# Output matmuls in one run per tile shape, and PSUM banks of their own for the first three chunks, in a linear-attention and two-layer MLP kernel

## The chip, the cores and the metric

The kernel runs on one core of a Trainium2 chip. The metric is the device time of one execution in microseconds (us); a lower time is better. Each figure for a whole kernel is the median of several executions. The profiles come from one execution each.

## The reference

Four batches of eight heads with 768 steps of 48 channels go through a gated linear recurrence. Its output, as 3072 tokens of 384 channels, goes through two gated MLPs with a width of 1536; the second normalizes its input first. Everything is float32.

```python
for t in range(S):
    state = alpha[:, :, t, :, None] * state + np.einsum('bhd,bhe->bhde', k[:, :, t], v[:, :, t])
    y[:, :, t] = np.einsum('bhd,bhde->bhe', q[:, :, t], state)
x = y.transpose(0, 2, 1, 3).reshape(B * S, H * D)
# first MLP
g = x @ w_gate;  x = (g * sigmoid(g) * (x @ w_val)) @ w_out
# second MLP: the same with its own weights, on x / rms(x) * rms_g
```

## The kernel before

**The recurrence in chunks.** The 768 steps of each of four batches are cut into six chunks of 128 steps: 24 chunks `n` in all, batch after batch within a step range, so that chunk `n` continues the state of chunk `n - 4`. A chunk works on all eight heads at once, as four pairs `p` with a half `h` each on partitions 0 to 63 and 64 to 127. Inside a chunk, the work goes by levels `LEVELS = (1, 2, 4, 8, 16, 32, 64)`, called l0 to l6 below. `merge` multiplies the decays into q and k in place on VectorE (DVE), level by level. `copy_qk` (ScalarE, ACT) copies what a level needs. `scores` (TensorE, PE) forms q k^T of a level as 16 matmuls with a tile of 64 rows and 32 columns. `masks` (DVE) and `copies_p` (ACT) bring the scores to SBUF. `outputs` adds, for each level, four matmuls with a tile of 128 rows and 32 columns and eight matmuls with a tile of 64 rows and 32 columns into the chunk's output in PSUM; chunks from n = 4 on also take in the old state that way (`Sd`, 128 rows; `Sc`, 64 rows). `own_terms` starts this output with three transposes of `yn`. For chunks up to n = 19, four transposes of k (into `kp`, copied to `kt` by ACT) and 16 matmuls in `kv` form the k^T v that `state` adds to the state. A matmul of float32 small tiles shows as two records in the trace. Chunks 0 to 5 use all levels, chunks from 6 on start at l2 and compute the first steps directly on DVE (`direct_ops`), which ends in `yn` after two DMAs through DRAM.

**Steps and slots.** A chunk has steps T = 0 to 19. A new chunk starts every 12 slots, so that step T of chunk n runs in the same slot as step T - 12 of chunk n + 1, and the older chunk comes first in the slot. In `chunk`, scores of l0 to l3 are at T = 6, masks of l0 to l2 at T = 7 and of l3 at T = 8, scores of l4 to l6 at T = 9, their masks and copies at T = 10, transposes of k at T = 12, their copy at T = 13, `own_terms` and the outputs of l0 to l3 at T = 14, `kv` and the outputs of l4 to l6 at T = 16, and `split_x` and `state` at T = 17 and 18. `split_x` writes the chunk's output from PSUM into the MLP's input (L375, L379 on ACT, L381 on DVE). Every engine runs its instructions in the order of this program.

**PSUM.** There are eight banks. Three are the tile `Y`, the others are `g`, `v`, `o0`, `o1` and `o2` of the MLP, one buffer each. The first 128 columns of the three banks of `Y` hold the chunk's output. The other columns hold the scores, the transposed k and k^T v of every chunk.

**The MLPs.** Tokens are in blocks of 3, 3, 3, 3, 4, 4 and 4 chunks in the first MLP and six blocks of 4 in the second. `mlp_points` walks over the blocks and over 12 slices f of the width; each (block, f) has three pieces: `g` (L612), `v` (L612) and `o` (L653), where `o` belongs to the slice before. Chunks 0 to 2 run before the first block, with T = 6 of chunk 3 ahead of the first `g`. After that, the slots of the chunks of the next block are spread over the pieces: one slot after each piece in blocks 0 to 2, four slots over three pieces in blocks 3 to 5. The last block of the first MLP and the second MLP have no chunks beside them.

**Weights.** They come as 64-bit words. For the first MLP, `conv` turns them into float32 in steps that are dealt out between the slots: ACT L152 and L158, DVE L159, L168 and L174 for each f. `splits` (ACT L189, DVE L193) splits them for the later blocks. The first block (0, 0) uses float32 matmuls (6 records a piece), the others three float32r products (9 records a piece).

Of the kernel before, what the change touches and what calls it, by code (L numbers as in the profile page):

```python
# [10 lines left out]
F32 = mybir.dt.float32  # L11
F32R = mybir.dt.float32r
I32 = mybir.dt.int32
AF = mybir.ActivationFunctionType
# [5 lines left out]
B, H, S, D = 4, 8, 768, 48  # L20
NT, DM, DFF = B * S, H * D, 1536
C = 128
NCB = S // C
NCH = B * NCB
NP = H // 2
CDS = (1,) * 6 + (4,) * (NCH - 6)
NX = 2
LEVELS = (1, 2, 4, 8, 16, 32, 64)
NL = len(LEVELS)
NF = DFF // 128  # L30
KT = DM // 128
BLOCKS = ((3, 3, 3, 3, 4, 4, 4), (4,) * 6)
MB = 4
NW = MB * C
# [21 lines left out]
class Kernel:  # L56


    def __init__(self, tc, ctx, qka, vl, vlx, vn, qn, dirx, w1, w2, g2, mask, ident, zero, out):
        self.tc, self.nc, self.ctx = tc, tc.nc, ctx  # L60
        self.d = dict(qka=qka, vl=vl, vlx=vlx, vn=vn, qn=qn, dirx=dirx, w=(w1.bitcast(I32), w2.bitcast(I32)), out=out)
        self.const = const = self.pool("const", 1)
        self.wp = self.pool("wp", NF)
        self.mp = self.pool("mp", 2)
        self.rp = self.pool("rp", 1)
        self.ps = self.pool("ps", 1, space=PSUM)
        self.Y = self.ps.tile([128, 3, NW], F32, name="Y")
        self.kvt = self.Y[:, 2, C:C + NP * D].rearrange("d (p e) -> d p e", e=D)
        self.kp = self.Y[:, 0:2, C:3 * C]
        self.dram = self.pool("dram", 1, space=DRAM)  # L70
        self.x2d = [self.dram.tile([128, KT, NW], F32, name=f"x2d{j}") for j in range(len(BLOCKS[1]))]

        self.actx = ExitStack()
        ac = self.pool("ac", 1, self.actx)
        self.a1 = self.pool("a1", 1, self.actx)
        self.a2 = self.pool("a2", 2, self.actx)
        self.qk = [ac.tile([128, 3, NP, C], F32, name=f"qk{i}") for i in range(2)]
        self.vlt = [ac.tile([128, NP, 64], F32, name=f"vl{i}") for i in range(NL - NX)]
        self.Sc = [ac.tile([128, NP, D], F32, name=f"S{b}") for b in range(B)]
        self.Sd = ac.tile([128, NP, 32], F32, name="Sd")  # L80
        self.pt32 = ac.tile([128, NP, 64], F32, name="pt32")
        self.mask = ac.tile([128, NL - 2, 64], F32, name="mask")
        self.ident = const.tile([128, 128], F32, name="ident")
        self.mask_d, self.ident_d, self.g2_d, self.zero_d = mask, ident, g2, zero
        self.W, self.X, self.P = {}, {}, {}
        self.vnt, self.dt, self.bpt, self.kc, self.kt, self.yn = {}, {}, {}, {}, {}, {}
        self.ydd = [self.dram.tile([128, 8 * D], F32, name=f"ydd{i}") for i in range(2)]
        self.later = []
# [164 lines left out]
        v = sub(self.qk[n % 2], b, [(NP * C - b, 2), (2 * b, NP * 64 // b), (1, b)])  # L253
        self.nc.scalar.activation(out=sub(t, 0, [(NP * 64, 2), (b, NP * 64 // b), (1, b)]), in_=v, func=AF.Copy)  # L254

    def place_sc(self, l):
        i, c = (l // 2, 1 + l % 2) if l < 4 else (l - 4, 3)
        return i, slice(c * C, c * C + C)

    def scores(self, n, ls):  # L260

        nc = self.nc
        qk = self.qk[n % 2]
        out = {}
        for l in ls:
            b = LEVELS[l]
            if b < CDS[n]:
                continue
            if b < 64:
                sc = out[l] = self.Y[:, *self.place_sc(l)].rearrange("s (p t) -> s p t", p=NP)  # L270
                kc = self.kc.pop((n, l))
                qc, kc = kc[:, 0], kc[:, 1]
            else:
                sc = out[l] = self.Y[:, 2, C:3 * C].rearrange("s (p t) -> s p t", p=NP)
                qc, kc = qk[:, 0, :, 64:128], qk[:, 1, :, 0:64]
            for p in range(NP):
                for g in range(2):
                    for h in range(2):
                        d = slice(64 * h, 64 * h + 64)
                        o = 64 * h + 32 * g  # L280
                        gs = slice(32 * g, 32 * g + 32)
                        nc.tensor.matmul(out=sc[o:o + 32, p], lhsT=kc[d, p, gs], rhs=qc[d, p, gs if b < 64 else slice(0, 64)],  # L282
                                         start=True, stop=True, skip_group_check=True)
        return out
# [27 lines left out]
            self.nc.tensor.matmul(out=self.Y[:, k, 0:C], lhsT=yn[:, C * k:C * k + C], rhs=self.ident, is_transpose=True,  # L312
                                  start=True, stop=False, skip_group_check=True)

    def outputs(self, n, ls, own=False):
        mm = lambda o, a, x: self.nc.tensor.matmul(out=o, lhsT=a, rhs=x, start=False, stop=False, skip_group_check=True)  # L316
        ls = [l for l in ls if LEVELS[l] >= CDS[n]]
        pt = {l: self.P.pop((n, l)) for l in ls}
        q = self.qk[n % 2][:, 0]

        def y(p, part, l=None):
            j = 3 * p + part
            t = self.Y[32 * (j % 4):32 * (j % 4) + 32, j // 4, 0:C]
            return t if l is None else t.rearrange("e (j u i) -> e j u i", u=2, i=LEVELS[l])[:, :, 1]
        own = own and n >= B
        if own:
            for p in range(NP):
                mm(y(p, 1), self.Sd[:, p], q[:, p])
        for l in ls:
            for p in range(NP):  # L330
                mm(y(p, 1, l), self.vlt[l][:, p, 32:64], pt[l][:, p])
        halves = [(p, h, slice(64 * h, 64 * h + 64)) for p in range(NP) for h in range(2)]
        if own:
            for p, h, d in halves:
                mm(y(p, 2 * h), self.Sc[n % B][d, p, 16 * h:16 * h + 32], q[d, p])
        for l in ls:
            for p, h, d in halves:
                mm(y(p, 2 * h, l), self.vlt[l][d, p, 0:32], pt[l][d, p])
        if n == CDS.index(4) - 1 and NL - 1 in ls:
            self.pxfree = True  # L340

    def kv(self, n):

        nc = self.nc
        kv = self.kvt
        kt, vn = self.kt.pop(n), self.vnt.pop(n)
        for p in range(NP):
            for h in range(2):
                for o in (64 * h, 64 * h + 32):
                    nc.tensor.matmul(out=kv[o:o + 32, p], lhsT=kt[:, p, o:o + 32], rhs=vn[:, p, h],  # L350
                                     start=False, stop=True, skip_group_check=True)
# [86 lines left out]
    def chunk(self, n, T):  # L438

        nc = self.nc  # L440
        more = n + B < NCH
        nxt = n + 1 if n + 1 < NCH else None

        if T == 12 and more:

            for p in range(NP):
                nc.tensor.transpose(out=self.kp[:, p // 2, C * (p % 2):C * (p % 2) + C], in_=self.qk[n % 2][:, 1, p],  # L447
                                    identity=self.ident)
        if T == 14:
            self.own_terms(n)  # L450
            self.outputs(n, range(4), own=True)
        if T == 16:
            if more:
                self.kv(n)
            self.outputs(n, range(4, NL))
        if T == 6:
            self.sc = self.scores(n, range(4))
        if T == 9:
            self.sc.update(self.scores(n, range(4, NL)))

        if T == 15 and n + 2 < NCH:
            self.load_qk(n + 2)
        if T == 17 and nxt:
            self.load_vn(nxt)
        if nxt:
            for l in {15: (0, 1, 2), 16: (3,), 17: (4,), 18: (5,), 19: (6,)}.get(T, ()):
                if LEVELS[l] >= CDS[nxt]:
                    self.load_vl(nxt, l)

# [9 lines left out]
        if 1 <= T <= 6:  # L479
            self.merge(n, LEVELS[T - 1])  # L480
            self.products(n, LEVELS[T])
        if T == 7:
            self.masks(n, self.sc, range(3))
        if T == 8:
            self.masks(n, self.sc, [3])
# [4 lines left out]
        if T == 11 and n >= B:  # L490
            for h in range(2):
                o = slice(64 * h, 64 * h + 64)
                nc.scalar.activation(out=self.Sd[o, :, 16 * h:16 * h + 16], in_=self.Sc[n % B][o, :, 32 - 32 * h:D - 32 * h], func=AF.Copy)
        if T == 13 and more:
            kt = self.kt[n] = self.a1.tile([128, NP, 128], F32, tag="kt", name="kt")
            nc.scalar.activation(out=kt.rearrange("s (i p) d -> s i (p d)", i=2), in_=self.kp, func=AF.Copy)
        if T == 1:
            self.direct = self.direct_ops(n)
        if 1 <= T <= 9:
# [322 lines left out]
```

## Time and profile before

| | |
|---|---|
| three runs, median (lowest to highest) | 1148.22 us (1146.27 to 1148.75) |
| the profiled execution's own time | 1148.09 us |
| span of its trace, first to last instruction | 1146.3 us |
| busy: PE, DVE, ACT | 1083.5, 654.6, 415.1 us |
| mean granted TensorE clock | 0.979 |

A row of a timeline gives the start, the length from the first start to the last end, the engine, the line, the operation, the tile out of and into which it goes, its shape and the number of records, and in brackets how long the engine stood idle before and which instruction it then waited for. "issue" there is time in which the engine waited for nothing that the trace shows. The ends of PE's matmuls are modelled, so distances between PE's starts say more than lengths.

### The profile page before, as it was taken

The numbers are of one execution on the slowest core, as the hardware profiler recorded it, in microseconds if no ns is written. First come the engines' busy times: TensorE is split into PE (matmuls) and PEld (weight loads), VectorE is DVE, ScalarE is ACT, GpSimd is POOL, SyncE is SP. The second block draws the span as 40 slices with busy tenths as digits, with TensorE's granted clock in tenths as the row PEclk, the third lists the DMA queues.
The fourth block names the chain that finished last, engine by engine and source line by source line (L and its number), as shares of the span: only waits on it lengthen the run. The fifth ranks groups of instructions, "written<-read, shape, count | busy, mean of one in ns | idle before, by whom it ended". The sixth has DMA issues, their size and how long they took to land.

```text
span 1146.3 us, 29415 instructions
## 1 busy us (share of the span) xinstructions
PE 1083.5 (95%) x12864; PEld 894.1 (78%) x12864; DVE 654.6 (57%) x1361; ACT 415.1 (36%) x749; POOL 46.6 (4%) x81
## 2 busy tenths in 40 slices
PE   2567999999999999999999999999999999999997
PEld 1444668999998987777878888888888888888886
DVE  4568866786777877676754886832423323233221
ACT  3446534443443343333334444422231232222212
POOL 2002100000000000000000000000000000000000
PEclk9769999999999999999999999999999999999999
DMA  8647524434445443434415324110000000100000
GB/s 254 171 124 239 174 71 117 120 94 122 116 115 127 128 138 103 120 104 132 113 52 180 124 97 166 42 55 1 28 28 1 28 28 1 55 1 1 28 1 28
DMA packets 56033, 103.89 MB, mean 91 GB/s; under 512 B 7392, under 2 KB 40672, under 8 KB 55904
## 3 DMA queue, kind: packets, MB, share of 16 engines
q1 hardware_dynamic: 50592, 80.37, 24.7%
q0 software_dynamic: 5312, 21.63, 5.6%
q8 instruction: 101, 1.65, 0.6%
q14 instruction: 28, 0.23, 0.1%
HBM read 89.00 MB, written 12.98 MB: 89 GB/s over the span
## 4 chain that ended last, share of the span: by engine, by line
PE 86%; DVE 3%; DMA 1%; ACT 1%; issue 1%; SPq 0%; DVEq 0%; ACTq 0%; POOLq 0%
PE o L653 25%; PE g L612 25%; PE v L612 25%; PE Y L316 4%; PE Y L282 3%; PE Y L350 1%; DVE x L168 1%; PE Y L312 1%; PE Y L447 1%; DMA yn<-ydd 1%; PE Y L551 0%; DVE qk L231 0%; DMA ydd<-yd 0%; PE Y L532 0%; ACT x L152 0%
## 5 line engine op out<-in xcount | busy, mean ns | idle before, releaser
L622 DVE TENSOR_TENSOR s<-s,v 128x512 f32<-128x512 f32 (+1 forms) x156 | 100.7, 646 | 352.0 <-PE v L612 347.6
L612 PE MATMUL g<-xhi,w 128*128 128x512 f32 (+1 forms) x864 | 282.6, 381 | 0.0
L612 PE MATMUL v<-xhi,w 128*128 128x512 f32 (+1 forms) x864 | 281.9, 380 | 0.0
L653 PE MATMUL o<-hh,w 128*128 128x512 f32 (+1 forms) x864 | 208.6, 376 | 0.0
L628 ACT ACTIVATE hh<-s 128x512 fp32r<-128x512 f32 (+1 forms) x144 | 87.2, 606 | 273.9 <-DVE s L622 273.8
L619 ACT ACTIVATE s<-g 128x512 f32<-128x512 f32 (+1 forms) x156 | 87.8, 563 | 267.4 <-PE g L612 248.1
L612 PEld LDWEIGHTS g<-xhi,w 128*128 128x128 f32 x864 | 161.2, 188 | 27.9
L612 PEld LDWEIGHTS v<-xhi,w 128*128 128x128 f32 x864 | 161.3, 188 | 27.0
L653 PEld LDWEIGHTS o<-hh,w 128*128 128x128 f32 x864 | 159.9, 188 | 25.8
L612 PE MATMUL g<-xlo,w 128*128 128x512 f32 (+1 forms) x432 | 162.7, 377 | 0.0
L612 PE MATMUL v<-xlo,w 128*128 128x512 f32 (+1 forms) x432 | 162.5, 376 | 0.0
L653 PE MATMUL o<-hl,w 128*128 128x512 f32 (+1 forms) x432 | 120.2, 386 | 0.6 <-ACT ev L573 0.4
L634 DVE TENSOR_TENSOR hl<-s,hh 128x512 fp32r<-128x512 f32 (+1 forms) x144 | 94.3, 655 | 40.9 <-ACT hh L628 37.5
L612 PEld LDWEIGHTS g<-xlo,w 128*128 128x128 f32 x432 | 81.2, 188 | 12.7
L612 PEld LDWEIGHTS v<-xlo,w 128*128 128x128 f32 x432 | 81.2, 188 | 12.3
L653 PEld LDWEIGHTS o<-hl,w 128*128 128x128 f32 x432 | 77.8, 188 | 15.4 <-ACT ev L573 1.1
L231 DVE TENSOR_TENSOR qk<-qk,bpb 128x512 f32<-128x512 f32 x96 | 65.6, 683 | 5.7 <-ACT kc L254 3.4
L254 ACT ACTIVATE kc<-qk 128x512 f32<-128x512 f32 x72 | 45.4, 631 | 60.2 <-DVE qk L231 59.4
L316 PE MATMUL Y<-pt,vl 64*32 64x64 f32 (+1 forms) x2880 | 55.5, 230 | 2.3 <-issue 2.3
L316 PEld LDWEIGHTS Y<-pt,vl 64*32 64x32 f32 (+1 forms) x2880 | 46.1, 112 | 6.4 <-issue 4.1
L282 PEld LDWEIGHTS Y<-kc 64*32 64x32 f32 x2304 | 25.8, 113 | 28.6 <-issue 14.4
L282 PE MATMUL Y<-kc 64*32 64x32 f32 x2304 | 31.4, 201 | 15.3 <-DVE pt L293 11.1
(103 smaller groups left out, 1031.0 us busy)
## 6 DMA issues: line engine op xcount, KB each, us to landing
vl<-vl SPq DMA_DIRECT2D x120, 128.0 KB, 4.1
qk<-qka SPq DMA_DIRECT2D x48, 288.0 KB, 4.9
room<-w POOLq DMA_DIRECT2D x36, 384.0 KB, 5.4
dir<-dirx SPq DMA_DIRECT2D x54, 192.0 KB, 3.2
wraw<-w SPq DMA_DIRECT2D x18, 384.0 KB, 3.8
room<-w SPq DMA_DIRECT2D x18, 384.0 KB, 4.0
vn<-vn SPq DMA_DIRECT2D x24, 192.0 KB, 3.8
x2in<-x2d SPq DMA_DIRECT2D x6, 768.0 KB, 4.1
```

Source lines behind the costliest of these rows:

```text
L168: nc.vector.scalar_tensor_tensor(out=xi, in0=xi, scalar=3, in1=lo, op0=ALU.logical_shift_left, op1=ALU.bitwise_or)
L231: self.nc.vector.tensor_tensor(out=v, in0=v, in1=sub(t, o, [(1, 2), (2, nb), (0, b)]), op=ALU.mult)
L254: self.nc.scalar.activation(out=sub(t, 0, [(NP * 64, 2), (b, NP * 64 // b), (1, b)]), in_=v, func=AF.Copy)
L282: nc.tensor.matmul(out=sc[o:o + 32, p], lhsT=kc[d, p, gs], rhs=qc[d, p, gs if b < 64 else slice(0, 64)], start=True, stop=True, skip_group ...
L312: self.nc.tensor.matmul(out=self.Y[:, k, 0:C], lhsT=yn[:, C * k:C * k + C], rhs=self.ident, is_transpose=True, start=True, stop=False, ski ...
L316: mm = lambda o, a, x: self.nc.tensor.matmul(out=o, lhsT=a, rhs=x, start=False, stop=False, skip_group_check=True)
L612: nc.tensor.matmul(out=ps[:, :N], lhsT=a, rhs=x, start=(q == 0), stop=(q == len(ops) - 1))
L619: nc.scalar.activation(out=s[:, :N], in_=g[:, :N], func=AF.Silu)
L622: nc.vector.tensor_tensor(out=s[:, :N], in0=s[:, :N], in1=v[:, :N], op=ALU.mult)
L628: nc.scalar.activation(out=hh[:, :N], in_=s[:, :N], func=AF.Copy)
L634: nc.vector.tensor_tensor(out=hl[:, :N], in0=s[:, :N], in1=hh[:, :N], op=ALU.subtract)
L653: nc.tensor.matmul(out=O[gj][i][:, :N], lhsT=a[:, 128 * i:128 * i + 128], rhs=x[:, :N], start=(f == 0 and q == 0), stop=(f == NF - 1 and q ...
```

## The change

The outputs are no longer split by level but by tile shape: part 0, at T = 14, holds every matmul with 128 rows of all levels, and `kv`, which also has 128 rows, runs in front of it; part 1, at T = 16, holds every matmul with 64 rows. The loads of the next chunks that overwrite what part 1 reads are issued from T = 17 on. Chunks 0 to 2 (`early`) take the MLP's banks `g`, `v` and `o0` for the scores of l0 to l3, the scores of l4 to l6 and the transposed k. The later chunks stay in `Y`, but use whole banks: the scores of l0 to l3 the third, those of l4 to l6 the first, the transposed k and k^T v the second. Scores of l0 to l3 go from T = 6 to T = 7 in these chunks, and their masks all to T = 8. The transposes of k go from T = 12 to 11 and their copy from T = 13 to 12 in all.

```diff
-        self.kvt = self.Y[:, 2, C:C + NP * D].rearrange("d (p e) -> d p e", e=D)
-        self.kp = self.Y[:, 0:2, C:3 * C]
...
-    def place_sc(self, l):
-        i, c = (l // 2, 1 + l % 2) if l < 4 else (l - 4, 3)
-        return i, slice(c * C, c * C + C)
+    def bank(self, n, i):
+        if n < BLOCKS[0][0]:
+            return self.ps.tile([128, NW], F32, tag=("v", "o0", "g")[i], name="early")
+        return self.Y[:, i]
...
+        bank = self.bank(n, 2 if ls[0] < 4 else 0)
...
-                sc = out[l] = self.Y[:, *self.place_sc(l)].rearrange("s (p t) -> s p t", p=NP)
+                sc = out[l] = bank[:, C * (l % 4):C * (l % 4) + C].rearrange("s (p t) -> s p t", p=NP)
...
-    def outputs(self, n, ls, own=False):
+    def outputs(self, n, part):
...
+        if part == 0:
+            if n >= B:
+                for p in range(NP):
+                    mm(y(p, 1), self.Sd[:, p], q[:, p])
+            for l in ls:
+                for p in range(NP):
+                    mm(y(p, 1, l), self.vlt[l][:, p, 32:64], self.P[n, l][:, p])
+            return
...
-        if T == 12 and more:
+        if T == 11 and more:
+            self.kp = self.bank(n, 1).rearrange("s (p d) -> s p d", p=NP)
...
         if T == 14:
             self.own_terms(n)
-            self.outputs(n, range(4), own=True)
-        if T == 16:
             if more:
                 self.kv(n)
-            self.outputs(n, range(4, NL))
-        if T == 6:
+            self.outputs(n, 0)
+        if T == 16:
+            self.outputs(n, 1)
+        early = n < BLOCKS[0][0]
+        if T == (6 if early else 7):
             self.sc = self.scores(n, range(4))
...
-        if T == 15 and n + 2 < NCH:
+        if T == (15 if n < B else 17) and n + 2 < NCH:
             self.load_qk(n + 2)
...
-            for l in {15: (0, 1, 2), 16: (3,), 17: (4,), 18: (5,), 19: (6,)}.get(T, ()):
+            for l in {17: (0, 1, 2), 18: (3, 4), 19: (5, 6)}.get(T, ()):
...
-        if T == 7:
+        if T == (7 if early else 8):
             self.masks(n, self.sc, range(3))
...
-        if T == 13 and more:
+        if T == 12 and more:
```

## Rows read from the trace of the kernel before

**Rows 1.** The page: busy tenths of PE in 40 slices of the span.

```profile
PE   2567999999999999999999999999999999999997
```

**Rows 2.** Windows of 100 us: busy us and records of PE, PEld, DVE, ACT, POOL; clock.

```profile
0.00:100.00 100.00, 52.01 (x1661) 37.93 (x1662) 62.61 (x121) 44.49 (x71) 15.94 (x33) 0.81 0.66 193
100.00:200.00 100.00, 93.44 (x1518) 63.38 (x1519) 74.49 (x141) 46.73 (x81) 8.48 (x14) 0.97 0.45 136
200.00:300.00 100.00, 99.60 (x1802) 93.59 (x1792) 75.66 (x183) 42.63 (x92) 5.21 (x8) 1.00 0.42 111
```

**Rows 3.** Waits of PE, whole span: us in total, times, longest.

```profile
PE Y L282 <- DVE pt L293: 11.1, 3, 5.8
...
PE Y L282 <- DVE xlo L381: 6.2, 2, 5.3
```

**Rows 4.** Timeline of PE, outputs of chunk 5 at T = 14.

```profile
167.59 0.41 PE L316 MATMUL Y<-px 128*32 128x64 f32 x16
167.81 0.41 PE L316 MATMUL Y<-pt,vl 128*32 128x64 f32 x16
168.15 0.45 PE L316 MATMUL Y<-qk,S 64*32 64x128 f32 x16
```

**Rows 5.** Timeline of PE, chunks 0 to 2.

```profile
22.54 0.66 PE L282 MATMUL Y<-kc 64*32 64x32 f32 x32 [5.80 <-DVE pt L293]
...
43.24 1.38 PE L282 MATMUL Y<-qk 64*32 64x32 f32 x51 [2.58 <-issue]
...
49.01 0.90 PE L312 MATMUL Y<-ident,yn 128*128 128x128 f32 x3 [1.11 <-ACT kt L496]
```

**Rows 6.** Timeline of DVE, chunks 0 to 3.

```profile
21.98 0.41 DVE L293 TENSOR_TENSOR pt<-Y,mask 128x256 f32<-128x256 f32 x1
...
24.53 0.42 DVE L293 TENSOR_TENSOR pt<-Y,mask 128x256 f32<-128x256 f32 x1 [0.42 <-PE Y L282]
...
35.55 0.36 DVE L357 COPY S<-Y 128x192 f32<-128x192 f32 x1 [0.99 <-ACT x L375]
...
44.66 0.42 DVE L293 TENSOR_TENSOR pt<-Y,mask 128x256 f32<-128x256 f32 x1 [3.85 <-PE Y L282]
...
55.67 0.36 DVE L357 COPY S<-Y 128x192 f32<-128x192 f32 x1 [2.57 <-ACT x L375]
...
63.88 0.43 DVE L293 TENSOR_TENSOR pt<-Y,mask 128x256 f32<-128x256 f32 x1 [1.00 <-PE Y L282]
...
75.62 0.36 DVE L357 COPY S<-Y 128x192 f32<-128x192 f32 x1 [2.98 <-ACT x L375]
...
79.35 0.76 DVE L293 TENSOR_TENSOR px<-Y,mask 128x256 f32<-128x256 f32 x2 [1.31 <-PE Y L282]
```

**Rows 7.** Timeline of ACT, output of chunk 1.

```profile
55.14 0.49 ACT L375 ACTIVATE x<-Y 128x384 f32<-128x384 f32 x1 [1.47 <-PE Y L316]
```

**Rows 8.** Timeline of PE, scores of chunks 4 and 5 in the first block.

```profile
113.55 1.08 PE L282 MATMUL Y<-px 64*32 64x32 f32 x64 [5.29 <-DVE xlo L381]
...
148.34 0.72 PE L282 MATMUL Y<-px 64*32 64x32 f32 x62 [0.92 <-DVE xlo L381]
...
149.56 2.20 PE L653 MATMUL o<-s,x 128*128 128x384 f32 x6
151.60 2.10 PE L612 MATMUL g<-x,x 128*128 128x384 f32 x6
```

**Rows 9.** Timeline of DVE around 148 us and in a block with 1.56 us pieces.

```profile
147.74 0.55 DVE L381 TENSOR_TENSOR xlo<-Y,xhi 128x384 fp32r<-128x384 f32 x1
...
162.88 0.55 DVE L622 TENSOR_TENSOR s<-s,v 128x384 f32<-128x384 f32 x1 [4.11 <-PE v L612]
...
376.71 0.42 DVE L293 TENSOR_TENSOR pt<-Y,mask 128x256 f32<-128x256 f32 x1
```

**Rows 10.** Timeline of PE, scores of l4 in the same block.

```profile
378.15 0.46 PE L282 MATMUL Y<-kc 64*32 64x32 f32 x32
```

**Rows 11.** The chain of waits, one piece there: start, length, what.

```profile
384.69 1.57 PE o L653 x9
```

More of the change, by code (lines that the diff above doesn't have):

```diff
@@ L273, in scores @@
             else:
-                sc = out[l] = self.Y[:, 2, C:3 * C].rearrange("s (p t) -> s p t", p=NP)
+                sc = out[l] = bank[:, 2 * C:4 * C].rearrange("s (p t) -> s p t", p=NP)
                 qc, kc = qk[:, 0, :, 64:128], qk[:, 1, :, 0:64]
@@ L313, in own_terms, with y @@
                                   start=True, stop=False, skip_group_check=True)
-    def outputs(self, n, ls, own=False):
+    def outputs(self, n, part):
         mm = lambda o, a, x: self.nc.tensor.matmul(out=o, lhsT=a, rhs=x, start=False, stop=False, skip_group_check=True)
-        ls = [l for l in ls if LEVELS[l] >= CDS[n]]
-        pt = {l: self.P.pop((n, l)) for l in ls}
+        ls = [l for l in range(NL) if LEVELS[l] >= CDS[n]]
         q = self.qk[n % 2][:, 0]
-        def y(p, part, l=None):
-            j = 3 * p + part
+        def y(p, i, l=None):
+            j = 3 * p + i
             t = self.Y[32 * (j % 4):32 * (j % 4) + 32, j // 4, 0:C]
             return t if l is None else t.rearrange("e (j u i) -> e j u i", u=2, i=LEVELS[l])[:, :, 1]
[L325 to L331, printed above, removed]
+        if part == 0:
[6 more added lines that the diff above has]
+            return
         halves = [(p, h, slice(64 * h, 64 * h + 64)) for p in range(NP) for h in range(2)]
-        if own:
+        if n >= B:
             for p, h, d in halves:
@@ L336, in outputs @@
         for l in ls:
+            pt = self.P.pop((n, l))
             for p, h, d in halves:
-                mm(y(p, 2 * h, l), self.vlt[l][d, p, 0:32], pt[l][d, p])
-        if n == CDS.index(4) - 1 and NL - 1 in ls:
+                mm(y(p, 2 * h, l), self.vlt[l][d, p, 0:32], pt[d, p])
+        if n == CDS.index(4) - 1:
             self.pxfree = True
@@ L344, in kv @@
         nc = self.nc
-        kv = self.kvt
+        kv = self.kvt = self.Y[:, 1, C:C + NP * D].rearrange("d (p e) -> d p e", e=D)
         kt, vn = self.kt.pop(n), self.vnt.pop(n)
@@ L442, in chunk @@
         nxt = n + 1 if n + 1 < NCH else None
-        if T == 12 and more:
+        if T == 11 and more:
+            self.kp = self.bank(n, 1).rearrange("s (p d) -> s p d", p=NP)
             for p in range(NP):
-                nc.tensor.transpose(out=self.kp[:, p // 2, C * (p % 2):C * (p % 2) + C], in_=self.qk[n % 2][:, 1, p],
-                                    identity=self.ident)
+                nc.tensor.transpose(out=self.kp[:, p], in_=self.qk[n % 2][:, 1, p], identity=self.ident)
         if T == 14:
             self.own_terms(n)
-            self.outputs(n, range(4), own=True)
-        if T == 16:
             if more:
                 self.kv(n)
-            self.outputs(n, range(4, NL))
-        if T == 6:
+            self.outputs(n, 0)
[3 more added lines that the diff above has]
+        if T == (6 if early else 7):
             self.sc = self.scores(n, range(4))
@@ L493, in chunk @@
                 nc.scalar.activation(out=self.Sd[o, :, 16 * h:16 * h + 16], in_=self.Sc[n % B][o, :, 32 - 32 * h:D - 32 * h], func=AF.Copy)
-        if T == 13 and more:
+        if T == 12 and more:
             kt = self.kt[n] = self.a1.tile([128, NP, 128], F32, tag="kt", name="kt")
-            nc.scalar.activation(out=kt.rearrange("s (i p) d -> s i (p d)", i=2), in_=self.kp, func=AF.Copy)
+            nc.scalar.activation(out=kt, in_=self.kp, func=AF.Copy)
         if T == 1:
```

## The prediction

> **What bounds the kernel now.** I read the page's slices first. PE is busy for nine tenths or more of the time from the seventh slice on, so from about 170 us [rows 1]. The windows of 100 us say the same with numbers: PE is busy 52.0 us of the first 100, 93.4 of the second and 99.6 of the third, where the granted clock is also 1.00, the 2.4 GHz level [rows 2]. From there on the kernel's end moves by what PE's own work costs. Nothing else matters unless PE has to wait for it. Before that it is the other way round: PE waits, and the question is for whom. The table of PE's waits puts most of it on line 282, the scores, which wait for masks on DVE (11.1 us in three places) and for the output's split on DVE (6.2 us in two) [rows 3].
>
> So there are two prices to find. One is what the order of the matmuls costs on PE after 150 us. The other is how much earlier PE gets busy for good. For the second I followed PE, DVE and ACT side by side through chunks 0 to 3. In this stretch, a chunk is a loop: scores, masks, next scores, next masks, next chunk's merges, the old chunk's output. DVE idles in it at few places only, and each of them is a row: 0.42, 3.85 and 1.00 us for PE's scores of l4 to l6 in chunks 0, 1 and 2; 0.99, 2.57 and 2.98 us for ACT's copy of the output; 1.31 us for chunk 3's first scores [rows 6]. ACT in turn stood 1.47 us waiting for PE's outputs of chunk 1 [rows 7].
>
> Then, up to 148 us, the first MLP block runs. DVE carries its weight conversion beside the chunks and hands over to ACT and back with few gaps; PE idles 5.29 us and 0.92 us before scores because `split_x` on DVE comes late [rows 8]. At 148.34 us that happens for the last time. By 162.88 us DVE waits 4.11 us for PE [rows 9]. So 148 us is the seam: an instruction stream of DVE and ACT that ends earlier there moves the whole rest of the kernel forward.
>
> **The switch of the tile shape.** In a chunk, PE goes from 128-row to 64-row tiles twice before the change, inside T = 14 and inside T = 16, and never after it: T = 14 then holds 128-row tiles only and T = 16 only 64-row tiles. Entering from the MLP's full tiles and leaving to them stays at two each. The price of one switch is in three starts: 16 records of 128-row tiles take 167.81 - 167.59 = 0.22 us up to the next 16 of the same shape, and these take 168.15 - 167.81 = 0.34 us up to the first 64-row tile [rows 4]. The switch costs 0.12 us. Two per chunk, in the 19 chunks 5 to 23 whose outputs lie behind the seam, make 2 x 19 x 0.12 = 4.6 us. Below, the bound is 0 (the gap could be the first weight load of any new run, paid again on leaving); above it is 0.15 us each, if the starts of such short runs scatter by a few hundredths: 5.7 us. I take 4.6, for the row measures this very step. The number of records does not change: `kv` and all matmuls are there as before.
>
> The Trainium skill (TensorEngine Tiling (Array Packing), Key Properties) says that changing the tiling mode drains the TensorE, which agrees with the gap; by the 128 cycles that its page TensorE: Matmul & The Clock Gate gives for a drain (step 4 of what each phase is for), an estimate at 2.4 GHz is 0.05 us a switch, and the sum would be 2.0 us in place of 4.6. The trace's 0.12 us decides.
>
> **The startup.** Here banks count. The scores of l4 went to the first bank, yet at 22.54 us they had waited 5.80 us for a mask [rows 5], and the mask that ended just then, at 22.39 us, was that of l3, which reads the second bank [rows 6]. So this kernel orders every access to `Y` as one tile. The Trainium skill (PSUM — Partial Sum Buffer, PSUM bank collisions raise a hardware error) asks for a guard by bank and quadrant only; by it the wait would have been for the two masks of the first bank alone, but l5 in the second bank would have stood until 22.39 us anyway. With `g`, `v` and `o0` as other tiles, chunks 0 to 2 lose these waits: scores of l4 to l6 no longer wait for masks, transposes of k not for `copies_p`, next scores not for the old state. Where DVE stood, what is late next?
>
> - Chunk 0: the 0.42 us wait goes; but `kt` now comes ahead of the next chunk's first copy on ACT, and DVE's next merge waits for that. I take 0.2 (0 to 0.42).
> - Chunk 1: 3.85 us at most. PE's scores would be early, but PE also ran out of instructions for 2.58 us inside them ("issue" at 43.24 [rows 5]); that stall can grow into the freed wait. If it keeps its place, little is left. Bounds 0.3 (what the mask leaves if the records after the stall start a little earlier) and 3.85; I take 1.5, nearer to the stall, as nothing in the change shortens it.
> - State of chunk 1: DVE waited 2.57 us for ACT, against 0.99 for chunk 0, where ACT was not waiting for PE. The difference, 1.58, is about the 1.47 that ACT waited for PE [rows 6, 7]. PE's outputs had started 1.11 us late because of `kt` [rows 5], which now comes a step earlier. I take 1.3 (0 to 1.58).
> - Chunk 2, masks: PE's scores have no stall inside, the 1.00 us goes whole (0.3 to 1.00).
> - State of chunk 2: 2.98 - 0.99 = 1.99 us at most; I take the 1.1 that `kt` explains (0 to 1.99).
> - Chunk 3: 1.31 us for scores that its masks, now at T = 8, meet one DVE operation later. I take 0.5 (0 to 1.31).
>
> Together 0.2 + 1.5 + 1.3 + 1.0 + 1.1 + 0.5 = 5.6 us, bounds 0.6 and 10.2. This shift of DVE and ACT should last to the seam, since in between they wait mostly for each other; weight loads are issued behind DVE's conversions and shift with them.
>
> **One piece at the seam.** At 148.34 us, PE waited for `xlo` with the scores of chunk 5 at its head and the `o` piece queued behind [rows 8]. After the change these scores stand at T = 7, behind that `o`. PE does the piece while it waits: 151.60 - 149.56 = 2.04 us [rows 8], which PE had idled away earlier. The same at 113.55 us (5.29 us idle) gives PE slack, but no time at the seam, where DVE's `xlo` ends the wait again. Bounds 0.9 (the idle seen there) and 2.1; I take 2.0.
>
> **Moved at no cost.** Behind the seam, masks at T = 8 must end before the scores of l4 at T = 9, with two pieces of PE between. In the tightest stretch (1.57 us pieces [rows 11]) the mask of l3 ended at 376.71 + 0.42 = 377.13 and the scores started at 378.15 [rows 9, 10]: 1.0 us in hand. The masks of l2 join it, but the direct operations that stood between go ahead of them, so the end stays. Loads of q and k move two slots later, with five pieces (5 x 1.57 = 7.9 us at the shortest) left before DVE needs them; other loads keep as much. If DMA were late, DVE would stand first and PE a step later.
>
> **The sum.** 4.6 + 5.6 + 2.0 = 12.2 us off 1148.09, the profiled execution's own time (span 1146.3 and 1.8 around it): 1135.9. The median of the runs shown is 0.13 higher, so 1136.0.
>
> **The rivals.**
>
> 1. The startup's gain is given back: PE's instruction supply, or conversions that wait for ACT, hold the seam where it is. For it: the 2.58 us "issue" stall; against it: DVE's gaps are rows that the change addresses. It leaves 4.6 us, or 5.5 with the 0.9 idle at the seam: 1143.
> 2. Switches give nothing, as the gap is paid again when the run leaves to full tiles from another shape. For it: ends are modelled, and no row shows 128-row tiles followed by the MLP. Then 5.6 + 2.0 are left: 1140.6.
> 3. Slower: the masks at T = 8 end after PE reaches T = 9. It makes the whole slower once they are later by more than the 1.0 us in hand plus 12.2 / 19 = 0.64 us a chunk. That happens if they land behind the product L622, which waits for `v`: then the scores wait for it and two masks, 0.55 + 2 x 0.42 = 1.4 us [rows 9] in each of 19 chunks, 26.6 - 12.2 = 14.4 us slower: 1162.6. Against it: T = 8 follows `g`, and L622 comes after `v`.
> 4. No change: the kernel's order doesn't reach the path at all. PE's 99.6 of 100 us speaks against it.
>
> **How the numbers follow.** I give the forecast 0.62, rival 1 0.15, rival 2 0.10, rival 3 0.05, rival 4 0.05, and 0.03 to a startup that gains near its upper bound. About 0.2% (2.3 us) is what a measurement of this kernel can tell from no change. Faster: 0.62 + 0.15 + 0.10 + 0.03, less a little where rival 1 and other losses meet, 0.88. Same 0.07, slower 0.05. The range goes from 1131.5 (startup 9, switches 5.5, piece 2.1) to 1143.5, which takes in rivals 1 and 2.
>
> **What would show it.** Right: PE's record of 64-row outputs as one run after T = 16 with no gap inside; chunk 5's scores at 148.34 - 5.6 = 142.7 us, with the `o` piece done before them; DVE's waits on PE's scores gone in chunks 0 and 2 and smaller in chunk 1. Wrong: "issue" stalls that grow in chunks 1 and 2; DVE waiting for ACT where it waited for PE; new waits of PE for L293 after 150 us; the window from 200 us on below 99 us busy.

## The result and the profile after

The changed kernel takes 1136.24 us (median of four runs, 1135.21 to 1137.22) where the kernel before, timed beside it, takes 1148.49 us. The ratio of the means is 0.9896, 95% interval 0.9878 to 0.9914, which is 11.9 us less. The predicted time was 1136.0 us. The span of the profiled execution fell from 1146.3 to 1133.4 us, by 12.9 us; the execution profiled after the change is the fastest of its four (1135.21 us).

The windows of 100 us of the profile after (columns as in [rows 2]):

```profile
0.00:100.00 100.00, 58.72 (x1782) 43.97 (x1783) 68.13 (x131) 48.78 (x77) 17.51 (x36) 0.81 0.73 214
...
300.00:400.00 100.00, 98.23 (x1998) 90.78 (x1987) 77.23 (x197) 41.72 (x96) 5.97 (x9) 1.00 0.44 121
```

In the first 100 us PE does 1782 records where it did 1661, at the same mean clock of 0.81 as before. The last row is a warning: from 300 us on PE idles 1.8 us in 100, where before it was 1.0 (99.0 busy), and its 98.23 lie under the 99 that the prediction named as a sign of being wrong.

DVE's timeline through chunks 0 to 3, the places of [rows 6] (L293 is now L294, L357 is L360), and `xlo` at the seam (L381 is L384):

```profile
24.54 0.42 DVE L294 TENSOR_TENSOR pt<-early,mask 128x256 f32<-128x256 f32 x1
35.94 0.36 DVE L360 COPY S<-Y 128x192 f32<-128x192 f32 x1 [0.99 <-ACT x L378]
...
41.67 0.42 DVE L294 TENSOR_TENSOR pt<-early,mask 128x256 f32<-128x256 f32 x1 [0.47 <-PE early L283]
51.93 0.36 DVE L360 COPY S<-Y 128x192 f32<-128x192 f32 x1 [1.41 <-ACT x L378]
...
59.07 0.42 DVE L294 TENSOR_TENSOR pt<-early,mask 128x256 f32<-128x256 f32 x1
69.63 0.36 DVE L360 COPY S<-Y 128x192 f32<-128x192 f32 x1 [1.29 <-ACT x L378]
...
139.65 0.55 DVE L384 TENSOR_TENSOR xlo<-Y,xhi 128x384 fp32r<-128x384 f32 x1
```

Start by start against [rows 6], the last mask of chunk 1 comes 2.99 us earlier, the state of chunk 1 3.74, the last mask of chunk 2 4.81, the state of chunk 2 5.99, and `xlo` at the seam (147.74 before [rows 9]) 8.09 us earlier. PE at the seam:

```profile
137.07 2.10 PE L656 MATMUL o<-s,x 128*128 128x384 f32 x6
140.25 0.72 PE L283 MATMUL Y<-px 64*32 64x32 f32 x62 [1.07 <-DVE xlo L384]
...
141.47 2.20 PE L615 MATMUL g<-x,x 128*128 128x384 f32 x6
```

The scores of chunk 5 start at 140.25 (148.34 in [rows 8]), with the `o` piece done ahead of them, and `g` follows at 141.47 (151.60 in [rows 8]). So the 12.9 us are 8.09 up to the scores at the seam, 10.13 - 8.09 = 2.04 for the piece, and 12.9 - 10.13 = 2.8 for all that lies behind. Of the 8.09, 0.7 is the start of the execution itself: the first scores wait 11.2 us for the first `px`, against 11.9. Chunk 0 loses that lead again, at a load for DVE's direct operations, first before, then after:

```profile
21.50 0.56 DVE L391 TENSOR_TENSOR dir<-dir 128x384 f32<-128x384 f32 x1 [0.65 <-DMA dir<-qn]
```

```profile
22.01 0.56 DVE L394 TENSOR_TENSOR dir<-dir 128x384 f32<-128x384 f32 x1 [1.84 <-DMA dir<-qn]
```

The load comes 0.5 us later although the execution started 0.7 earlier, and the last mask of chunk 0 starts where it did before (24.54 and 24.53). The waits of PE in the first 150 us of the kernel before, and in the whole span of the kernel after:

```profile
PE Y L282 <- ACT px L254: 12.7, 2, 11.9
PE Y L282 <- DVE pt L293: 11.1, 3, 5.8
...
PE Y L282 <- issue: 5.1, 3, 2.6
...
PE Y L316 <- issue: 2.3, 2, 1.8
```

```profile
PE early L283 <- ACT px L252: 12.0, 2, 11.2
PE early L450 <- DVE qk L229: 8.8, 3, 4.8
PE early L283 <- issue: 7.2, 4, 2.7
...
PE Y L318 <- issue: 4.1, 2, 2.5
PE Y L450 <- ACT pt L307: 2.5, 6, 1.0
```

The waits of the scores for masks (11.1 us) are gone. PE now waits for DVE's merge of k (`qk`, 8.8 us) ahead of the transposes. "Issue", time in which PE waits for nothing that the trace shows and which I take for a lack of instructions, has grown from 7.4 to 11.3 us. And the later chunks' transposes wait for the last copy of `pt`, five of six times behind the seam; before, the transposes had such waits (L447, 6.5 us) in the startup alone.

### The profile page after: what moved, and what is told of

Its sections match the earlier page's. It is cut to its first block, busy times and chain, and to the rows that moved or that the text cites. A ratio compares the mean times of both kernels' runs of the same rounds, so it can differ in the third digit from the quotient of the medians.

```text
span 1133.4 us, 29415 instructions
## 1 busy us (share of the span) xinstructions
PE 1077.9 (95%) x12864; PEld 892.8 (79%) x12864; DVE 655.3 (58%) x1361; ACT 415.2 (37%) x749; POOL 46.5 (4%) x81
## 4 chain that ended last, share of the span: by engine, by line
PE 86%; DMA 2%; ACT 1%; DVE 1%; issue 0%; SPq 0%; ACTq 0%; DVEq 0%
PE g L615 26%; PE v L615 25%; PE o L656 25%; PE Y L318 4%; PE Y L283 3%; DMA x2d<-ev 1%; PE Y L353 1%; PE Y L450 1%; ACT pt L304 1%; PE Y L313 1%; PE Y L554 0%; PE Y L535 0%; ACT ev L576 0%; DVE pt L294 0%; DMA vl<-vl 0%
## 5 line engine op out<-in xcount | busy, mean ns | idle before, releaser
L318 PE MATMUL Y<-pt,vl 64*32 64x64 f32 (+1 forms) x2880 | 46.7, 229 | 4.1 <-issue 4.1
L318 PEld LDWEIGHTS Y<-pt,vl 64*32 64x32 f32 (+1 forms) x2880 | 42.7, 111 | 4.6 <-issue 4.6
L229 DVE TENSOR_TENSOR qk<-qk,bpa 128x512 f32<-128x512 f32 x48 | 32.9, 686 | 4.2 <-ACT px L252 2.5
L283 PEld LDWEIGHTS Y<-kc 64*32 64x32 f32 x2016 | 21.6, 110 | 12.8 <-issue 7.5
```

The source lines that it names most:

```text
L229: self.nc.vector.tensor_tensor(out=v, in0=v, in1=sub(t, o, [(1, 2), (2, nb), (0, b)]), op=ALU.mult)
```

## The experiments

Ratios are to the kernel before, timed beside each kernel on the same chip. For what lies behind the seam, one window serves for all kernels, from the first transpose of `yn` of chunk 5 to the end of the span (columns as in [rows 2]: from and to, length, PE busy and its records, and so on). It holds 10278 records of PE in every kernel. Before, and then after:

```profile
166.92:1146.30 979.38, 971.12 (x10278) 818.97 (x10276) 538.08 (x1152) 336.58 (x625) 23.44 (x36) 1.00 0.26 76
```

```profile
156.89:1133.40 976.51, 966.68 (x10278) 816.09 (x10276) 539.84 (x1153) 336.43 (x625) 23.45 (x36) 1.00 0.26 77
```

So behind the seam PE's work shrank by 4.4 us, and its idle time grew from 8.3 to 9.8 us.

How much one trace can tell is seen where programs are the same. Behind the seam, the kernel before, banks_only, bank_scores and bank_kp run the same program; their windows take 979.4, 982.0, 978.9 and 979.7 us, with PE busy for 971.1 to 971.5. Up to the seam, the changed kernel, kp_mid, after_ev3 and kp_mid_ev3 run the same program; from ACT's first copy (`px`) to the scores of chunk 5 they take 128.3 to 131.1 us. So a difference of less than about 3 us between two such spans is not shown by one pair of traces. PE's busy time and short stretches of chunks scatter less.

### The sorted order alone: sort_only

```diff
 the kernel before, with outputs(n, part) of the change, its later loads, and
...
         if T == 14:
             self.own_terms(n)
+            if more:
+                self.kv(n)
+            self.outputs(n, 0)
         if T == 16:
+            self.outputs(n, 1)
```

> The kernel before with only the outputs sorted by tile shape (k^T v and 128-row tiles at T = 14, 64-row tiles at T = 16, loads from T = 17 on); banks and all other steps as before. Theory (two switches less per chunk are worth 0.33 us a chunk behind the seam, nothing ahead of it): chunk 5's scores stay at 148 us, within 1 us, and the time falls by 19 x 0.33 = 6 us less what moved loads cost, to 1142 to 1144 us. Rival (the order of the matmuls is worth nothing, the banks and the earlier steps bring everything): 1148 us.

Measured: 1141.32 us, ratio 0.9942 (0.9930 to 0.9954). Its window behind the seam:

```profile
165.28:1137.90 972.62, 965.12 (x10278) 816.70 (x10276) 539.44 (x1152) 335.76 (x625) 23.42 (x36) 1.00 0.26 77
```

The order alone takes 979.38 - 972.62 = 6.8 us off what lies behind the seam, more than the 4.6 of the prediction, and more than the whole change keeps there (2.9). PE's busy time shrinks by 971.12 - 965.12 = 6.0 us of these. Ahead of the seam, the scores of chunk 5 start at 146.71 us, 1.6 earlier than before, where they were to stay within 1 us; one trace doesn't tell that from scatter. The size per chunk is seen in a quiet chunk of a block with 512 columns, first before, then after:

```profile
504.27 0.49 PE L312 MATMUL Y<-ident,yn 128*128 128x128 f32 x3
...
506.06 0.50 PE L612 MATMUL g<-xhi,w 128*128 128x512 f32 x1
...
508.32 0.55 PE L350 MATMUL Y<-vn,kt 128*32 128x48 f32 x32
...
509.79 0.50 PE L612 MATMUL v<-xhi,w 128*128 128x512 f32 x1
```

```profile
492.06 0.49 PE L313 MATMUL Y<-ident,yn 128*128 128x128 f32 x3
...
493.73 0.50 PE L615 MATMUL g<-xhi,w 128*128 128x512 f32 x1
...
496.00 0.45 PE L318 MATMUL Y<-qk,S 64*32 64x128 f32 x16
...
497.26 0.50 PE L615 MATMUL v<-xhi,w 128*128 128x512 f32 x1
```

The two bursts take 1.79 + 1.47 = 3.26 us before and 1.67 + 1.26 = 2.93 after: 0.33 us a chunk, 6.3 in 19 chunks. Two switches at 0.12 make 0.24 of the 0.33; what the rest is was not separated.

### The banks alone: banks_only

```diff
 the kernel before, with bank() of the change for n < 3 in scores and transposes;
 all steps, all later chunks and the outputs as before
```

> The kernel before with only the banks of chunks 0 to 2 changed (scores and transposed k in g, v and o0); all steps at their old places. Theory (waits of the startup are those for the one tile Y): chunk 5's scores come 5 to 7 us earlier than 148.3 us, and the time falls by as much, to about 1142 us. Rival (it is the earlier copy of the transposed k that brings the startup forward): at most 2 us, 1146.5 us.

Measured: 1142.10 us, ratio 0.9952 (0.9940 to 0.9964). PE at the seam:

```profile
141.16 0.72 PE L289 MATMUL Y<-px 64*32 64x32 f32 x62 [0.95 <-DVE xlo L388]
...
142.38 2.20 PE L662 MATMUL o<-s,x 128*128 128x384 f32 x6
```

The scores come 148.34 - 141.16 = 7.2 us earlier, with first scores at the same place as before (11.9 us): the startup's gain is that of the banks. The `o` piece still stands behind the wait. Behind the seam nothing is gained; 982.0 us are even 2.6 more in the same program, half of it one wait of 1.4 us for the copy of an output piece, which is scatter. The two halves multiply to 0.9942 x 0.9952 = 0.9894, and the whole change has 0.9896. That doesn't prove that the two add up to it, as the piece at the seam and the earlier transposes are in neither half.

### Two more switches: kv_between

```diff
 the changed kernel, with k^T v out of T = 14 and into the run of 64-row tiles:
             for p, h, d in halves:
                 mm(y(p, 2 * h, l), self.vlt[l][d, p, 0:32], pt[d, p])
+            if l == 5 and n + B < NCH:
+                self.kv(n)
```

> The changed kernel with k^T v (128 rows) moved from T = 14 into the middle of the 64-row run at T = 16: two more switches of tile shape in chunks 0 to 19, with the same matmuls. Theory (0.12 us a switch): 15 chunks behind the seam x 2 x 0.12 = 3.6 us longer, 1139.8 us, and the run at T = 16 shows two gaps of about 0.1 us around k^T v. Rival (a switch costs nothing, the shorter bursts come from something else): 1136.2 us.

Measured: 1137.66 us, ratio 0.9913 (0.9900 to 0.9926), some 1.4 to 2 us more than the changed kernel, where 3.6 were expected. In PE's timeline the run of 64-row tiles is now cut:

```profile
497.93 0.77 PE L318 MATMUL Y<-pt,vl 64*32 64x64 f32 x48
498.64 0.55 PE L355 MATMUL Y<-vn,kt 128*32 128x48 f32 x32
499.12 0.45 PE L318 MATMUL Y<-pt,vl 64*32 64x64 f32 x32
```

From chunk 6 to chunk 11 five chunks take 125.40 us against 124.26 in the changed kernel, 0.23 us a chunk for two switches, so 0.12 each, as the prediction read it. In the block after these, they cost nothing (85.95 us from chunk 12 to chunk 16 against 86.05). So the price holds where PE is the bound, and the block of the shortest pieces isn't bound by PE alone.

### Scores of the later chunks at T = 6: scores_t6

```diff
-        if T == (6 if early else 7):
+        if T == 6:
             self.sc = self.scores(n, range(4))
...
-        if T == (7 if early else 8):
+        if T == 7:
             self.masks(n, self.sc, range(3))
```

> The changed kernel with the scores of l0 to l3 at T = 6 and the masks of l0 to l2 at T = 7 in all chunks, as before the change. Theory (at the seam PE does one o piece while it waits for the split on DVE): chunk 5's scores start at about 140.2 us as in the changed kernel, but the o piece then follows them, and the time is 2.0 us longer, 1138.2 us. Rival (the piece is hidden anyway): 1136.2 us.

Measured: 1141.07 us, ratio 0.9937 (0.9925 to 0.9949): 4.7 us more than the changed kernel, for a piece of 2.0. PE's timeline at the seam, and the window of the piece behind the wait (from and to, length, PE busy and its records, granted clock, DMA share, GB/s):

```profile
141.40 0.72 PE L283 MATMUL Y<-px 64*32 64x32 f32 x62 [2.03 <-DVE xlo L384]
...
142.69 3.77 PE L656 MATMUL o<-s,x 128*128 128x384 f32 x6
146.29 2.10 PE L615 MATMUL g<-x,x 128*128 128x384 f32 x6
```

```profile
142.69:146.29 3.60, 3.60 (x10) 0.56 0.02 5
```

`g` comes 146.29 - 141.47 = 4.8 us later than in the changed kernel. Of these 1.15 are scores that come later (the execution's own start is 0.9 late), and 3.60 are the piece, which runs at a granted clock of 0.56 on the mean, mostly at the 1.2 GHz level, after PE had stood idle for 2.03 us. In the changed kernel, PE idles 1.07 us at the same place and does `g` in 2.04 us. So moving the scores behind `o` bought the piece, and 1.6 us of clock that in the kernel before were not at stake (0.92 us idle, the piece in 2.04 [rows 8]).

The 1.6 us are those of one trace, and the length of the idle time alone doesn't decide them. At the scores of chunk 4 PE idles longer in every kernel. The next piece, `g`, took 4.00 us at a granted clock of 0.50 after 3.35 us of idle in the changed kernel, but 2.04 us at 1.00 after 3.36 us in kv_between. The scores there, and the window of `g`, first in the changed kernel, then in kv_between:

```profile
106.23 1.08 PE L283 MATMUL Y<-px 64*32 64x32 f32 x64 [3.35 <-DVE xlo L384]
...
108.10:112.10 4.00, 4.00 (x14) 0.50 0.72 268
```

```profile
105.95 0.72 PE L283 MATMUL Y<-px 64*32 64x32 f32 x62 [3.36 <-DVE xlo L386]
...
107.17:109.21 2.04, 2.04 (x14) 1.00 0.98 306
```

### One bank at a time: bank_scores and bank_kp

```diff
 banks_only, with bank() for
+  the scores of chunks 0 to 2 alone (bank_scores)
+  the transposes of k of chunks 0 to 2 alone (bank_kp)
```

> The kernel before with only the scores of chunks 0 to 2 in g and v; the transposed k stays in Y, all steps as before. Theory (the wait that counts is that of Y's accesses for the scores and their masks; with the scores elsewhere, the transposes in Y have nothing recent to wait for either): as with all three banks, chunk 5's scores at 141 to 142 us and 1142 us in all. Rival (the transposed k's bank has a part of its own): 1 to 2 us longer.

> The kernel before with only the transposed k of chunks 0 to 2 in o0; scores stay in Y. Theory (masks and scores carry most of the startup): only the state's waits shrink, chunk 5's scores come 1 to 2.5 us earlier, 1146 us. Rival (the transposed k carries it): 1142 us.

Measured: bank_scores 1143.29 us, ratio 0.9967 (0.9954 to 0.9980); bank_kp 1142.92 us, ratio 0.9964 (0.9951 to 0.9976). Waits of PE in the first 150 us, bank_scores first:

```profile
PE early L289 <- issue: 8.4, 4, 4.1
...
PE Y L319 <- ACT kt L505: 7.0, 5, 2.1
```

```profile
PE Y L289 <- DVE pt L300: 11.9, 3, 6.5
```

Relative to the first scores, the seam comes 5.0 us earlier with the scores' banks and 5.8 with the transposes' bank, against 7.2 with both; that the one brings more than the other is within scatter. My expectation for the second was far too low. There the scores wait for masks as long as before (11.9 us), yet PE's lack of instructions during the scores (5.1 us before) has all but gone (0.2). With the scores' banks the masks' waits are gone, but lack of instructions (8.4 us) and `kt` (7.0 us) have taken their place. The waits stand in for one another; PE's table of waits doesn't tell what removing one of them brings.

What the lack of instructions follows is seen in the records that PE has done when a stall ends. Windows from 0 to the end of a stall, one of before and one of after (PE's records in brackets):

```profile
0.00:43.22 43.22, 13.15 (x604) 0.94 0.83 242
```

```profile
0.00:40.23 40.23, 13.73 (x603) 0.92 0.86 253
```

Before, the five stalls end at 604, 860, 988, 1243 and 1371 records; after, those of more than 1 us end at 476, 603, 858, 986 and 1240, and two of 0.2 us at 222 and 1368 (some records are missing from a trace). So the places are the same in both orders, 128 or 256 apart. In the traces of the twelve other kernels, every stall of the first 90 us ends at one of these counts, within three records. The same record is passed at 43.22 and at 40.23 us, so the stall of chunk 1 moved 3.0 us forward with the work ahead of it.

### The transposes one step later: kp_t12

```diff
-        if T == 11 and more:
+        if T == (11 if early else 12) and more:
             self.kp = ...
-        if T == 12 and more:
+        if T == (12 if early else 13) and more:
             kt = ...
```

> The changed kernel with the transposes of k and their copy back at T = 12 and 13 for chunks from 3 on (chunks 0 to 2 keep T = 11 and 12). Theory (part of what the sorted tiles save behind the seam is given back because the transposes, one step earlier, meet the copies of the scores on ACT): PE's waits for L307 behind the seam, 1.4 us, are gone, the chunks 12 to 15 are up to 0.5 us shorter each, and the time is 1.4 to 2.4 us shorter, 1134 to 1135 us. Rival (what is given back there belongs to the moved loads or to instruction supply): 1136 us, with new waits in the same chunks.

Measured: 1136.50 us, ratio 0.9905 (0.9890 to 0.9920), no change. Two rows point to why, the window behind the seam and PE's wait for `kt`:

```profile
160.06:1134.30 974.24, 965.54 (x10278) 816.34 (x10276) 539.41 (x1152) 336.07 (x625) 23.50 (x36) 1.00 0.26 77
```

```profile
PE Y L313 <- ACT kt L499: 4.2, 2, 2.9
```

Behind the seam it is 976.51 - 974.24 = 2.3 us less, and PE's waits for L307 are gone there. Ahead of it, the transposes of `yn` of chunks 3 and 4 wait for `kt`, and chunk 5's outputs come 2.1 us later, counted from the first scores. Each of the two differences is within the scatter of a trace, but the wait for `kt` stands again in kp_t12_ev3 (4.1 us), and the next section sets more traces beside the other. As they stand, the early step pays ahead of the seam and costs behind it.

### A third output buffer, and the two steps split: kp_t12_ev3, kp_mid, kp_mid_ev3, after_ev3, ev3_only

```diff
 kp_mid: transposes and copy early for n < 6, late for later chunks
+        if T == (11 if n < 6 else 12) and more:
+        if T == (12 if n < 6 else 13) and more:
 ..._ev3: kp_t12, kp_mid, the changed kernel and the kernel before with
-        t = self.rp.tile([128, NW], F32, tag="ev", name="ev", bufs=2)
+        t = self.rp.tile([128, NW], F32, tag="ev", name="ev", bufs=3)
```

> The same with three buffers in place of two for the output pieces on their way to DRAM. Theory (at a block's change PE's first o piece waits for the third copy, which waits for a store to land): the waits of PE for the copy of o, 1.2 us in the changed kernel, are gone, 1133 to 1134.5 us. Rival (stores are only late by chance): the same time as with two buffers.

> The changed kernel, with the transposes of k and their copy at T = 11 and 12 for chunks 0 to 5 and at T = 12 and 13, their old steps, for the later chunks. Theory: with all transposes from chunk 3 on at their old steps, the time was unchanged because two effects cancel: 2.3 us less behind the first outputs of chunk 5 (transposes no longer meet ACT's copies) and about 2.1 us more ahead of it (PE waits 4.2 us for kt). Split at chunk 6, only the first is left: the outputs of chunk 5 start at the changed kernel's place within 0.5 us, PE has next to no waits of the transposes for copies behind them, and the time is 1134.0 us (1133 to 1135). Rival: the lateness of chunk 5 has another cause than kt, and the gain behind it is only the catching up of that lateness: 1136.3 us, as the changed kernel.

> The same as kp_mid with three buffers in place of two for the MLP's output on its way to DRAM (ev). Theory: the two edits act at different places and add: 3.8 us less than kp_mid, 1130.2 us (1129 to 1131.5), with no wait of PE's o piece for ev. Rival: the third buffer's gain overlaps with that of the transposes, as both take away stalls of the same pieces: 1132.5 us, no better than the three buffers with all late transposes.

> The changed kernel with three ev buffers and nothing else. Theory: the buffer's gain does not depend on where the transposes stand: 3.8 us less than the changed kernel, 1132.4 us (1131.5 to 1133.5). Rival: it does, because a stall taken away at the stores makes PE meet ACT's copies more often in front of the transposes: 1134.5 us or more.

> The kernel before with three ev buffers and nothing else. Theory: the stall at the output stores was there before the change as well and is no loss that the change brought: 3 to 4 us less than before, 1144 us. Rival: the changed order moved the stores into the stall, and before had next to none (its trace shows 0.4 us of PE waiting for ev): within 1 us of before, 1147.5 us.

| kernel | median us | ratio | behind the seam, us |
|---|---|---|---|
| kp_t12_ev3 | 1132.66 | 0.9871 (0.9854 to 0.9889) | 970.70 |
| kp_mid | 1135.26 | 0.9891 (0.9876 to 0.9907) | 975.03 |
| kp_mid_ev3 | 1128.95 | 0.9841 (0.9826 to 0.9855) | 970.33 |
| after_ev3 | 1131.78 | 0.9864 (0.9850 to 0.9877) | 973.36 |
| ev3_only | 1144.73 | 0.9976 (0.9967 to 0.9985) | 977.23 |

ACT's waits for the landing of an output store and PE's for `ev`, in the kernel before, whole span:

```profile
ACT ev L573 <- DMA x2d<-ev: 5.0, 6, 1.7
...
PE o L653 <- ACT ev L573: 0.4, 1, 0.4
```

In the four kernels with three buffers both are gone. The stall at the stores is older than the change: a third buffer takes 2.5 us off the kernel before, where PE showed 0.4 us of waiting for `ev`. It takes 3.7 us off the changed kernel (1148 x (0.9896 - 0.9864)). So the rival, that the change alone had put the stores into the stall, falls. That the change made it worse isn't shown: 2.5 and 3.7 us lie within each other's intervals, ACT waits 6.7 us for stores in both kernels, and PE's wait for `ev` grew from 0.4 to 1.2 us.

Split at chunk 6, the transposes brought nothing that can be measured with two buffers (0.9891 beside 0.9896, where 1134.0 us were expected), and 2.8 us with three (kp_mid_ev3 beside after_ev3, whose single runs don't overlap). In kp_mid, ACT waits 8.3 us for stores where the changed kernel has 5.0, and the startup came 0.8 us worse in chunk 1, which no edit touches there: its stall at record 604 took 3.0 us in place of 2.2. Which of these took the gain of 1.5 us behind the seam was not settled. With three buffers the place of the gain is plain. Chunks 11 to 16, first after_ev3, then kp_mid_ev3, and the transposes of one chunk in after_ev3:

```profile
306.94:417.10 110.16, 107.37 (x2139) 97.24 (x2138) 84.67 (x219) 46.09 (x104) 6.50 (x10) 1.00 0.48 130
```

```profile
308.35:415.44 107.09, 106.33 (x2140) 97.57 (x2139) 84.24 (x217) 45.72 (x104) 6.50 (x10) 1.00 0.50 134
```

```profile
367.37 0.66 PE L450 MATMUL Y<-ident,qk 128*128 128x128 f32 x4 [0.28 <-ACT pt L307]
```

All of the difference behind the seam (973.36 - 970.33 = 3.0 us) lies in these five chunks, the block with the shortest pieces, 2.0 of them as idle time of PE, of which 1.4 are the transposes' waits for L307 in after_ev3. The same five chunks take 109.7 to 110.2 us in the four kernels with sorted outputs and the early step (the changed kernel, kv_between, scores_t6, after_ev3), and 107.1 to 108.4 us in the five with the old step there (sort_only, kp_t12, kp_t12_ev3, kp_mid, kp_mid_ev3). The means are 2.4 us apart, and no trace of one group reaches the other. A step earlier, the transposes stand behind a copy of `copies_p` on ACT; a step later they don't. They write the second bank of `Y` and that copy reads the first, so here, too, they wait because `Y` is ordered as one tile.

kp_mid_ev3 is the fastest kernel of this study: 18.2 us less than before.

## Why the prediction held, step by step

**What bounds the kernel.** Right: the edits that moved the seam or shortened PE's work behind it moved the end, as far as the scatter of about 3 us in a trace lets it be seen. It was too simple for chunks 11 to 16, where PE's work and ACT's copies bound it together.

**The switch.** The mechanism was right and its price, 0.12 us, was measured again by kv_between. The term was too small: sorting saves 0.33 us a chunk and not 0.24, 6.3 us by the bursts and 6.8 by sort_only, above the bound of 5.7. Rival 2 (switches give nothing) falls by sort_only. What the 0.09 us a chunk beyond the two switches are stays open. As to the drain on a change of tiling mode of which the Trainium skill tells (TensorEngine Tiling (Array Packing), Key Properties), the estimate of 2.0 us for all chunks, from the 128 cycles of its page TensorE: Matmul & The Clock Gate, is under a third of the 6.8 us that sort_only shows.

**The startup.** 8.1 us at the seam, 7.4 counted from the first scores, against 5.6 predicted with bounds of 0.6 and 10.2. From the starts, term by term (predicted in brackets): chunk 0 together -0.4 us, or -1.1 counted from the first scores (0.2), masks of chunk 1 3.4 (1.5), state of chunk 1 0.75 (1.3), masks of chunk 2 1.1 (1.0), state of chunk 2 1.2 (1.1), chunk 3 up to its `xlo` 1.3 (0.5), and from there to the seam 0.8 (0). In chunk 0, the late load took the 0.7 us of the earlier start, and the copy `kt` ahead of the next chunk's first copy, which the prediction had named, the 0.4. The mis-sized term is that of chunk 1: the stall did not keep its place, as I had supposed, but came 3.0 us earlier with the record at which it happens. Rival 1 falls, though its sign, "issue" that grows, was there: 7.4 to 11.3 us. By itself that sign meant nothing, since the stalls then stood in time in which PE had waited for masks before.

**The piece.** 2.04 us against 2.0, as worked out. In scores_t6 it was worth more, as the granted clock fell behind 2.03 us of idle time there; kv_between shows that it need not fall.

**Moved at no cost.** This is the step that failed. For masks at T = 8 and the loads it held: no wait of PE for a mask is left behind the seam, and rival 3 falls. But the transposes of k, which I had counted in the startup alone, are also a step earlier in all later chunks, and meet ACT's copies there: 2.4 us between the means of the nine traces, 2.7 and 3.0 with three buffers (kp_t12_ev3 and kp_mid_ev3 beside after_ev3). The whole account behind the seam is 979.38 - 976.51 = 2.9 us: 6.8 from the order, less 2.4 for the transposes, less 1.5 that was not isolated and lies within the scatter of a trace. The prediction's 4.6 was too small for the gain and too large for what remained of it.

So the sum of 12.2 came out at 12.9 in the spans, in part by luck, because the startup was 2.5 us better and what lies behind the seam 1.8 us worse. Rival 4 (no change) falls with all of these runs.

## What to carry to other kernels

When a step is moved for the startup, cost it in every stage in which it is moved: here the same edit won about 2 us in one stage and lost as much in the next. A condition on the chunk number kept both once the output stores were out of the way (2.8 us with three buffers, nothing measurable with two). Waits in a table aren't additive: by the medians, removing either of two brought some three quarters of what both did, so the time that a wait holds is a bound, to be tried by removing it. And an engine that shows 0.4 us of waiting can still lose 2.5 us to stores that land late: there ACT waited 6.7 us for them. How this reaches PE was not traced.

## What was unexpected of the hardware

While PE runs small matmuls, it stalls at fixed counts of its records, 128 or 256 apart in all orders tried, for up to 4.1 us each. The stalls move with the work ahead of them. The trace has about as many weight loads as matmuls, so 128 matmul records stand for some 256 instructions. That would fit instructions that arrive in blocks, but no run tested it.

After 2.03 us of idle PE the granted clock of the next piece was 0.56 and the piece took 3.60 us in place of 2.04; after 1.07 us of idle at the same place it was 1.00 throughout. At an earlier place, 3.35 us of idle were followed by 0.50 in one kernel, and 3.36 us by 1.00 in another.
